# Moving the states' products of a chunked linear attention to another place in the loop, with one PSUM bank shared by sums and outputs

## The chip, the core and the metric

The kernel is one program on one core of a Trainium2 chip. The core has five engines that run side by side: TensorE (PE in the profile; its weight loads are PEld), VectorE (DVE), ScalarE (ACT), GpSimd (POOL) and SyncE (SP), which here issues nearly all DMAs. TensorE writes its results to PSUM, which has eight banks of 512 float32 columns on 128 partitions; DVE and ACT read them from there. The metric is the device time of one execution in microseconds, as the median of several runs.

## The reference

Three stages follow one another. The first is a linear attention with a decay for each token and feature, for 4 batches, 8 heads, 768 tokens and 48 features a head:

```python
for t in range(S):
    state = alpha[:, :, t, :, None] * state + np.einsum('bhd,bhe->bhde', k[:, :, t], v[:, :, t])
    y[:, :, t] = np.einsum('bhd,bhde->bhe', q[:, :, t], state)
```

Its output, as 3072 tokens of 384 features, goes through a soft mixture of 8 experts with 4 slots each (softmax of `x @ phi` over the tokens, `slot_input = d.T @ x`, relu between `w1` and `w2` for each expert, and back to the tokens by a softmax over the slots), and that through a gated MLP with 1536 hidden units (`silu(g) * val @ w_out`). The three MLP matrices arrive as float64 and are made into float32 on the chip, bit by bit.

## The kernel before

**Tiling.** Two heads make a unit, s = 0 on partitions 0 to 63 (48 of them used) and s = 1 on partitions 64 to 111. 4 batches of 4 units give 16 units, each cut into two groups h = 0 and h = 1 of three chunks of 128 tokens. The main loop (`fast`, from L622) runs over these 32 groups g. Within a chunk the attention is a masked product of queries and keys; what came earlier enters through a 48x48 state for each head. A group of h = 0 has no state for its first chunk, so it has 4 products with states, one of h = 1 has 6.

**One round of the loop**, in the order in which PE gets its work (the order is written by hand, the semaphores are set by the framework):

1. `emit_st(g, 1-h)` (L402, L404), a link of the chain of states: the identity times the last state is added on PE to the chunk's sum k'v, and ACT multiplies it with the chunk's total decay into the next state, in SBUF.
2. `emit_s(g+1)` (L353): scores of the next group, into two banks of their own.
3. `emit_st(g, 2-h)`: the second link. Each link needs the state that ACT made from the one before.
4. `emit_kt(g+1)` (L371) transposes the keys, and ACT copies them (L374).
5. `emit_xt(g-1)` (L462) transposes the outputs of the group before; ACT copies them (L466). Then `emit_masks(g+1)`: DVE (L360), ACT (L362) and POOL (L363) mask the scores.
6. `emit_l(g-1)` (L453): logits of the experts' slots from those outputs.
7. `emit_past(g)` (L420): the states times the queries, into the bank `y`, one column range of 128 for each chunk. The two heads lie on diagonal quarters of the array: rows 0 to 63 to columns 0 to 63, rows 64 to 111 to columns 64 to 111.
8. `emit_dh(g+1)` (L390): the chunks' sums k'v of the next group, into one of the three banks `m`. With an odd g, `emit_st(g+1, 0)` follows at once; it is ACT's multiplication alone.
9. `emit_ip(g)` (L432): masked scores times v, added onto the same bank `y`; ACT copies all 384 columns to SBUF as x (L434).

Every float32 product stands as two instructions in the trace, so a row with x12 is six products.

**Beside it** DVE and POOL make the decays three groups ahead (L306 to L325), ACT and DVE turn one piece of the float64 weights into float32 in most rounds (`conv_y`, L249 on ACT; `conv`, L253 to L261 on DVE), and after a batch's last unit the slot steps run (`slot_steps`, from L468): a peak on DVE, exponentials on ACT, two transposes and the slots' input on PE, in the rounds that follow.

**Loads.** SP works off one queue in order. Each round it loads keys, queries, decays and values of later groups; a load of the weights w1, then w2, then wo is issued while a credit lasts (840 columns a round, a tile of w1 or w2 is 1536) and while the allocator `Arena` has room. The arena has a part "near" (31600 columns) and a part "far" (19184). A buffer that is no longer needed at the end of the loop goes back to the arena, and neighbours that are free together hold a weight tile. Behind the loop come the last slot steps, the experts' first layer (L853), which frees the w1 tiles, the second layer (L910), which needs all of w2, and the MLP (L1006 to L1045).

PSUM's eight banks are `m` three times, `s` twice, and `y`, `l` and `r` once.

Of the kernel before, what the change touches and what calls it, by code (L numbers as in the profile page):

```python
# [8 lines left out]
F32 = mybir.dt.float32  # L9
# [9 lines left out]
CH = 128  # L19
# [3 lines left out]
NU = H // 2  # L23
NE, NSL, FE = 8, 32, 1024
# [7 lines left out]
BLK = 1536  # L32
SEL = {0: 2, 1: 3, 3: 4, 4: 5}
LAST = 4
GV0, RATE = 1, 840
TINY = 2.0 ** -55
NEAR, ROUND = 31600, 19184
LA = 3


# [52 lines left out]
def attention_slots_mlp(ctx: ExitStack, tc: tile.TileContext, kq, at, vt, phi, w1, w2, wgv, wo, cst, out):  # L93
    nc = tc.nc
# [9 lines left out]
    mask = cs[:, 128:256]  # L104
    sel = cs[:, 256:288]
    negm = cs[:, 288:289]
    phs = const.tile([112, NU, NSL], F32, name="phs")
    tots = const.tile([112, B * NU, NC], F32, name="tots")
    pall = const.tile([96, 385], F32, name="pall")
    nmx = const.tile([96, 4], F32, name="nmx")  # L110
# [30 lines left out]
    def program(general):  # L141
# [13 lines left out]
        z_g = zone(2, 2 * GP, 0)  # L155
        z_c = [(ar.alloc(GP, 0), GP)]

        zn = {nm: [0] * n for nm, n in (("a", 4), ("p", 5), ("v", 4), ("w", 2), ("x", 2))}
        zsize = {"a": HW, "p": HB, "v": 288, "w": HW, "x": 384}
        for z in "a0 a1 p2 a2 p3 v0 w0 a3 p4 v1 w1 p0 v2 p1 v3 x0 x1".split():  # L160
            zn[z[0]][int(z[1])] = ar.alloc(zsize[z[0]], 1)
        z_a, z_p, z_v, z_w, z_x = (zn[nm] for nm in "apvwx")
        z_y = zone(1, 5 * XK)
# [15 lines left out]
        def psm():  # L179
            return ps_m.tile([128, 512], F32, tag="m", name="m")  # L180
# [196 lines left out]
        def new_g():  # L377
            ng[0] += 1
            return gsts[:, ng[0] % 7, :]

        def emit_dh(g):
            n, h = sgs[g]
            vv[g] = have.pop(("v", g))
            v = view(vv[g]).rearrange("p (c e) -> p c e", e=96)
            t = ktok.pop(g)
            dps[g] = psm()
            for c in range(nk(g)):
                for s in range(2):
                    m = 64 if s == 0 else 48
                    nc.tensor.matmul(dps[g][64 * s:64 * s + m, c * 48:c * 48 + 48], lhsT=t[:, c, 64 * s:64 * s + m], rhs=v[:, c, 48 * s:48 * s + 48], start=(c == 0), stop=True, skip_group_check=True)  # L390

        dps = {}


        def emit_st(g, c):
# [9 lines left out]
            if c == nk(g) - 1:  # L405
                del dps[g]

        yps = {}


        def emit_past(g):
            n, h = sgs[g]
            q = view(qp[g], 112)
            yps[g] = ps_y.tile([128, 512], F32, tag="y", name="y")
            for c in range(3):
                cc = 3 * h + c
                o = slice(c * CH, (c + 1) * CH)
                for s in range(2) if cc else ():
                    p = slice(0, 64) if s == 0 else slice(64, 112)
                    nc.tensor.matmul(yps[g][p, o], lhsT=gst[n, cc][p, 0:p.stop - p.start], rhs=q[p, o], start=(cc == max(1, 3 * h)), stop=False, skip_group_check=True)  # L420
            del qp[g]
            release(pair.pop(g), z_p, g + 5)

        def emit_ip(g):
            n, h = sgs[g]
            v = view(vv[g]).rearrange("p (c e) -> p c e", e=96)
            ps = yps[g]
            for c in range(3):
                o = slice(c * CH, (c + 1) * CH)
                for s in range(2):  # L430
                    p = slice(0, 64) if s == 0 else slice(64, 112)
                    nc.tensor.matmul(ps[p, o], lhsT=v[:, c, 48 * s:48 * s + p.stop - p.start], rhs=smk[g, s][:, c], start=False, stop=True, skip_group_check=True)  # L432
            xt[g] = (z_x.pop(0), 384)
            nc.scalar.copy(view(xt[g], 112), ps[0:112, 0:384])  # L434
            del smk[g, 0], smk[g, 1], yps[g]
            release(vv.pop(g), z_v, g + 4)

        def release(r, z, g):
            if g < NSG:
# [5 lines left out]
        def emit_l(g):  # L445
            n, h = sgs[g]
            b, u = units[n]
            if u == 0 and h == 0:
                lps[b] = ps_l.tile([128, 512], F32, tag="l", name="l")
            x = view(xt[g], 112)  # L450
            for j in range(3):
                t0 = j * CH
                nc.tensor.matmul(lps[b][32 * j:32 * j + 32, CH * h:CH * h + CH], lhsT=phs[:, u, :], rhs=x[:, t0:t0 + CH], start=(u == 0 and h == 0), stop=(u == NU - 1), skip_group_check=True)  # L453

        def emit_xt(g, between=lambda: None):
            n, h = sgs[g]
# [11 lines left out]
        def slot_steps(b):  # L468
# [27 lines left out]
            def e_tok():  # L496
# [3 lines left out]
                st["et"] = st["e2"][:, 0:192].rearrange("p (r e) -> p r e", r=2)  # L500
                nc.vector.tensor_copy(st["et"].rearrange("p r e -> p (r e)"), ps[:, 0:192])

            def part(between=lambda: None):
                ps = psm()
                o = NU * b % 5
                pieces = [(0, o, min(NU, 5 - o))] + [(5 - o, 0, NU - 5 + o)] * (o > 1)
                for r in range(2):
                    if r:
                        between()
                    for u, p, w in pieces:  # L510
                        for j in range(3):
                            nc.tensor.matmul(ps[32 * j:32 * j + 32, 96 * u:96 * u + 96 * w], lhsT=st["et"][:, r, 32 * j:32 * j + 32], rhs=xtok[:, p:p + w, 3 * r + j, :], start=(r == 0 and u == 0), stop=(r == 1), skip_group_check=True)
                if own:
                    for c in (slice(0, 128), slice(128, 384)):
                        nc.scalar.copy(pb[:, c], ps[0:96, c])
                else:
                    nc.vector.scalar_tensor_tensor(out=pall[:, 0:384], in0=pall[:, 0:384], scalar=fac, in1=ps[0:96, 0:384], op0=ALU.mult, op1=ALU.add)
                    nc.vector.scalar_tensor_tensor(out=pall[:, 384:385], in0=pall[:, 384:385], scalar=fac, in1=den, op0=ALU.mult, op1=ALU.add)
                if b == B - 1:
                    drop((z_y[0], 5 * XK))  # L520
# [56 lines left out]
        def fast():  # L577
# [11 lines left out]
            calm, cold[0] = cold[0], view((z_g[0], 256)).bitcast(BF16)  # L589
            nc.gpsimd.memset(cold[0], 0.0)  # L590

            keep_warm(10)
            cold[0] = calm
            nc.vector.memset(rst, 0.0)
            nc.vector.memset(least, TINY)
# [9 lines left out]
            scan_w(1)  # L605
            scale(1, 0, nc.gpsimd)
            scan_p(1)
            keep_warm(4)
            scale(1, 1, nc.vector)
            emit_masks(0)  # L610
            emit_dh(0)
# [4 lines left out]
            scale(2, 0, nc.gpsimd)  # L616
            scale(2, 1, nc.vector)
            pump_units()
            keep_warm(6)
            pend = []  # L620
            credit[0] = 0
            for g in range(NSG):  # L622
                n, h = sgs[g]
                nxt = g + 1 < NSG

                emit_st(g, 1 - h)
                if GV0 < g and (g <= 8 or g % 8 not in (3, 4)):
                    conv_y()
                if g + 3 < NSG:
                    scan_w(g + 3, lambda: conv(0))  # L630
                    scan_p(g + 3)
# [12 lines left out]
                if g:  # L644
                    emit_xt(g - 1)
                if nxt:
                    emit_masks(g + 1)
                    del kp[g + 1]
                    pump_units()
                late = False  # L650
                if g:
                    emit_l(g - 1)
                    release(xt.pop(g - 1), z_x, g + 1)
                    p = sgs[g - 1][0]
                    if sgs[g - 1][1] == 1 and units[p][1] == NU - 1:
                        pend += slot_steps(units[p][0])
                        late = True
                        pend.pop(0)()
                if pend and not late:
                    pend.pop(0)()  # L660
                emit_past(g)
                if nxt:
                    emit_dh(g + 1)
                    if h:
                        emit_st(g + 1, 0)
                conv(2)
                emit_ip(g)
                if late:
                    pend.pop(0)()
                    pend.pop(0)()  # L670
                if gvd[0] == NG and z_c:
                    done_c()

                pump_gv()
                credit[0] = min(credit[0] + RATE, 2 * BLK)
                reserve[0] = 6 - len(gvb)
                while credit[0] > 0:
                    c = credit[0]
                    pump(1)
                    if credit[0] == c:  # L680
                        break
                pump_units()
            for r in z_t:
                drop(r)
            assert few[1] is not None
# [443 lines left out]
def _arrays(q, k, v, alpha, moe_phi, moe_w1, moe_w2, moe2_w_gate, moe2_w_val, moe2_w_out):  # L1129
# [14 lines left out]
        for i in range(NC):  # L1144
            at[:, :, 64 * s:64 * s + 48, 129 * i + 1:129 * i + 129] = a[:, :, s, :, i]
    vt = c(v.reshape(B, NU, 2, NC, CH, D).transpose(0, 1, 4, 3, 2, 5)).reshape(B, NU, CH, NC * 96)
    ph = np.zeros((112, NU, NSL), np.float32)
    pr = moe_phi.reshape(NU, 2, D, NSL)
    for s in range(2):
        ph[64 * s:64 * s + 48] = pr[:, s].transpose(1, 0, 2)  # L1150
# [31 lines left out]
```

## Time and profile before

| | |
|---|---|
| median of 3 runs | 389.02 us (388.72 to 393.24) |
| the profiled execution, its own time | 390.72 us |
| its span in the trace | 389.0 us |
| mean granted clock of TensorE | 0.987 |
| main loop, first to last scores after the start | about 24 to 148 us |
| experts and the last loads of w2 | about 156 to 188 us |
| MLP | about 199 to 382 us |

The span is the time from the first to the last instruction of the program in the trace. Each engine's rows give start and duration; PE's matmuls are pipelined, so that the row of one stage reaches into the next, and the distance from the start of a stage to the start of the next is the time that it costs. A value in square brackets behind a row is the idle time of the engine before it, and what ended it.

### The profile page before, as it was taken

The page shows a single profiled execution, that of the slowest core. Times are in us where ns is not written, and L with a number is a line of the kernel's source. Part 1 is how long each engine was busy: PE and PEld are TensorE (multiplying, and loading weights), DVE is VectorE, ACT ScalarE, POOL GpSimd, SP SyncE. Part 2 cuts the span into 40 slices and gives each one's busy share as a digit, 9 for nine tenths or more (in the row PEclk, how much of TensorE's full clock was granted, in tenths as well). Part 3 has the DMA queues.
Part 4 walks back from the last instruction along what each step waited for, and adds up shares of the span by engine and source line. Part 5 has one row for each costly group of instructions (what it writes and reads, how often), then busy time and mean ns, then how long its engine had stood idle before and what let it go on. Part 6 is the DMA issues. An engine that isn't in the chain of part 4 may idle for free.

```text
span 389.0 us, 8609 instructions
## 1 busy us (share of the span) xinstructions
PE 371.4 (95%) x3308; PEld 278.9 (72%) x3309; DVE 291.2 (75%) x566; ACT 201.2 (52%) x468; POOL 100.8 (26%) x105
## 2 busy tenths in 40 slices
PE   7799999999999999899899999999999999999992
PEld 3577777777777776434368868888888888888881
DVE  6969997999999973215789987677777867877550
ACT  2256665666456565523376755445455545446441
POOL 3347875685588641010300000000000000000000
PEclk9879999999999999999999999999999999999998
DMA  8969999899899959899900004204204114112002
GB/s 273 352 221 329 373 352 356 289 340 345 275 346 363 336 164 354 298 345 412 401 30 0 3 27 125 73 3 150 71 2 153 40 33 152 37 36 82 3 1 90
DMA packets 28627, 74.25 MB, mean 191 GB/s; under 512 B 3216, under 2 KB 11648, under 8 KB 28576
## 3 DMA queue, kind: packets, MB, share of 16 engines
q1 hardware_dynamic: 28256, 73.27, 53.3%
q8 instruction: 28, 0.46, 0.5%
q10 hardware_dynamic: 272, 0.21, 0.2%
q14 instruction: 23, 0.19, 0.2%
q0 software_dynamic: 48, 0.13, 0.1%
HBM read 68.87 MB, written 4.72 MB: 189 GB/s over the span
## 4 chain that ended last, share of the span: by engine, by line
PE 81%; DVE 6%; DMA 3%; ACT 2%; issue 2%; POOL 1%; SPq 0%; DVEq 0%; ACTq 0%; POOLq 0%
PE m L1045 22%; PE acc L1045 11%; PE s L353 6%; PE y L432 6%; PE y L420 6%; PE s L1006 4%; PE m L402 4%; PE s L1007 4%; PE m L390 3%; PE m L371 3%; PE l L453 3%; DMA near<-w 3%; PE s L853 3%; PE m L462 2%; DVE near L1012 1%
## 5 line engine op out<-in xcount | busy, mean ns | idle before, releaser
L1045 PE MATMUL m<-rnd 128*128 128x512 f32 x432 | 129.2, 389 | 0.0
L1045 PEld LDWEIGHTS m<-rnd 128*128 128x128 f32 x432 | 81.1, 188 | 16.8
L1009 ACT ACTIVATE near<-s 128x512 f32<-128x512 f32 x72 | 43.1, 599 | 79.0 <-PE s L1006 77.3
L1045 PE MATMUL acc<-rnd 128*128 128x512 f32 x216 | 81.1, 392 | 0.7 <-DVE rnd L901 0.7
L325 POOL TENSOR_TENSOR far<-far 112x384 f32<-112x384 f32 x61 | 74.5, 1240 | 8.8 <-DVE far L307 4.7
L1012 DVE TENSOR_TENSOR near<-near,s 128x512 f32<-128x512 f32 x72 | 49.3, 685 | 36.1 <-ACT near L1009 35.9
L1020 DVE TENSOR_TENSOR rnd<-near,rnd 128x512 fp32r<-128x512 f32 x72 | 49.4, 686 | 3.2 <-ACT rnd L1018 3.1
L1045 PEld LDWEIGHTS acc<-rnd 128*128 128x128 f32 x216 | 40.5, 188 | 10.3 <-DVE rnd L901 1.6
L1018 ACT CAST rnd<-near 128x512 fp32r<-128x512 f32 x72 | 44.3, 616 | 0.2 <-DVE near L1012 0.2
L404 ACT ACTIVATE far<-m,tots 112x48 f32<-112x48 f32 x80 | 24.3, 304 | 26.7 <-PE m L402 14.6
L307 DVE TENSOR_TENSOR_SCAN far<-far,r 112x388 f32<-112x388 f32 x32 | 30.8, 962 | 5.1 <-DMA far<-at 2.4
L353 PE MATMUL s<-far 64*128 64x128 f32 x384 | 30.8, 293 | 3.5 <-POOL far L325 2.2
L363 POOL TENSOR_SCALAR_AFFINE_SELECT far<-far 128x384 f32<-128x384 f32 x32 | 20.2, 631 | 47.3 <-ACT far L362 47.3
L1116 DVE TENSOR_REDUCE amm<-near 112x1 f32<-112x768 f32 x32 | 30.3, 946 | 2.5 <-DMA near<-at 2.5
L314 DVE TENSOR_TENSOR_SCAN far<-far,r 112x387 f32<-112x387 f32 x32 | 30.7, 959 | 1.1
L257 DVE SCALAR_TENSOR_TENSOR near<-near 128x384 uint32<-128x384 uint32 x36 | 21.6, 599 | 11.3 <-ACT near L249 10.3
L434 ACT COPY far<-y 112x384 f32<-112x384 f32 x32 | 15.3, 480 | 28.3 <-PE y L432 28.3
L353 PEld LDWEIGHTS s<-far 64*128 64x128 f32 x384 | 24.7, 191 | 6.1 <-POOL far L325 4.5
L432 PE MATMUL y<-far 128*48 128x128 f32 (+1 forms) x384 | 28.9, 276 | 0.0
L1006 PE MATMUL s<-rnd 128*128 128x512 f32 x72 | 28.3, 393 | 0.0
L1007 PE MATMUL s<-rnd 128*128 128x512 f32 x72 | 28.1, 391 | 0.0
L420 PE MATMUL y<-far 48*48 48x128 f32 (+1 forms) x320 | 24.9, 283 | 0.0
(163 smaller groups left out, 493.4 us busy)
## 6 DMA issues: line engine op xcount, KB each, us to landing
near<-w SPq DMA_DIRECT2D x18, 768.0 KB, 7.3
far<-kq SPq DMA_DIRECT2D x32, 384.0 KB, 5.1
far<-w SPq DMA_DIRECT2D x14, 768.0 KB, 6.3
near<-wgv SPq DMA_DIRECT2D x24, 384.0 KB, 5.8
far<-at SPq DMA_DIRECT2D x32, 194.0 KB, 5.0
near<-at SPq DMA_DIRECT2D x16, 339.1 KB, 3.3
far<-vt SPq DMA_DIRECT2D x32, 144.0 KB, 4.6
near<-wo SPq DMA_DIRECT2D x12, 384.0 KB, 8.0
```

Source lines behind the costliest of these rows:

```text
L307: nc.vector.tensor_tensor_scan(w[:, ::-1], a[:, ::-1], rst[:, ::-1], 0.0, ALU.mult, ALU.add)
L325: eng.tensor_tensor(out=xv, in0=xv, in1=sv, op=ALU.mult)
L353: nc.tensor.matmul(sps[g][s][:, o:o + CH], lhsT=k[64 * s:64 * s + 64, t0:t0 + CH], rhs=q[64 * s:64 * s + 64, t0:t0 + CH], start=True, stop ...
L420: nc.tensor.matmul(yps[g][p, o], lhsT=gst[n, cc][p, 0:p.stop - p.start], rhs=q[p, o], start=(cc == max(1, 3 * h)), stop=False, skip_group_ ...
L432: nc.tensor.matmul(ps[p, o], lhsT=v[:, c, 48 * s:48 * s + p.stop - p.start], rhs=smk[g, s][:, c], start=False, stop=True, skip_group_check ...
L1006: nc.tensor.matmul(pg, lhsT=swk[n][:, 128 * o:128 * o + 128], rhs=ctT[t % 4], start=True, stop=True)
L1007: nc.tensor.matmul(pv, lhsT=swk[n][:, 256 + 128 * o:256 + 128 * o + 128], rhs=ctT[t % 4], start=True, stop=True)
L1009: nc.scalar.activation(sg, pg, AF.Silu)
L1012: nc.vector.tensor_tensor(out=h_, in0=sg, in1=pv, op=ALU.mult)
L1018: nc.scalar.copy(hi, h_)
L1020: nc.vector.tensor_tensor(out=lo, in0=h_, in1=hi, op=ALU.subtract)
L1045: nc.tensor.matmul(p, lhsT=passes[j][0][:, sl], rhs=passes[j][1], start=(f == 0 and j == 0), stop=(f == NF - 1 and j == 2))
```

## The change

The products with the states move. Instead of standing between the logits and the next group's sums in round g, `emit_past(g)` now stands in round g+1, right behind the first link `emit_st(g+1, ...)`, and ahead of the scores. `emit_ip` now comes first and opens the output, `emit_past` adds to it and ends with the copies to SBUF.

The middle chunk of each group (c = 1) gets its output in a bank `m` of its own, with the two heads swapped: head 0 goes from rows 0 to 63 to columns 64 to 111, head 1 from rows 64 to 111 to columns 0 to 63. Chunks 0 and 2 stay in the bank `y`. ACT copies the output to x with two instructions (128 and 256 columns) instead of one. What reads x undoes the swap: the logits take a second copy of phi with the heads swapped, the slots' input reads the two heads in the other order.

The chunks' sums k'v (`dps`), which had a bank `m`, now lie in columns 256 to 399 of the same bank `y` that takes the outputs of the group before.

Besides: one buffer for x instead of two (the far part is 128 columns smaller, since phi's second copy takes 128 columns elsewhere); the conversion of weights starts in round 1 instead of 2; and once the units' loads are all issued, the credit for weight loads is no longer 840 a round but without limit; the warming matmuls use a bank `m`.

```diff
-GV0, RATE = 1, 840
+RATE = 840
-NEAR, ROUND = 31600, 19184
+NEAR, ROUND = 31600, 19056
...
+        def new_y():
+            ybank[0] = ps_y.tile([128, 512], F32, tag="y", name="y")
+            return ybank[0]
...
-            dps[g] = psm()
+            dps[g] = new_y()[:, 256:400]
...
+        def swap(c):
+            return int(c == 1 and not general)
+        def half(s):
+            return slice(0, 64) if s == 0 else slice(64, 112)
+        def y_out(g, s, c):
+            return yps[g][c == 1][half(s ^ swap(c)), CH * (c // 2):CH * (c // 2) + CH]
+        def emit_ip(g):
+            cleared = g + 1 < NSG
+            yps[g] = ybank[0] if cleared else new_y(), psm()
+            v = view(vv[g])
+            for c in range(3):
+                for s in range(2):
+                    o = y_out(g, s, c)
+                    e = 96 * c + 48 * s
+                    nc.tensor.matmul(o, lhsT=v[:, e:e + o.shape[0]], rhs=smk[g, s][:, c], start=(c == 1 or c == 0 and not cleared), stop=True, skip_group_check=True)
+            del smk[g, 0], smk[g, 1]
+            release(vv.pop(g), z_v, g + 4)
...
         def emit_past(g):
             n, h = sgs[g]
             q = view(qp[g], 112)
-            yps[g] = ps_y.tile([128, 512], F32, tag="y", name="y")
             for c in range(3):
                 cc = 3 * h + c
                 for s in range(2) if cc else ():
+                    o = y_out(g, s, c)
+                    nc.tensor.matmul(o, lhsT=gst[n, cc][half(s), 0:o.shape[0]], rhs=q[half(s), c * CH:(c + 1) * CH], start=False, stop=True, skip_group_check=True)
+            xt[g] = (z_x.pop(0), 384)
+            x = view(xt[g], 112)
+            y, z = yps.pop(g)
+            nc.scalar.copy(x[:, CH:2 * CH], z[0:112, 0:CH])
+            nc.scalar.copy(x.rearrange("p (c t) -> p c t", t=CH)[:, 0::2], y[0:112, 0:2 * CH].rearrange("p (c t) -> p c t", t=CH))
             del qp[g]
             release(pair.pop(g), z_p, g + 5)
...
                 emit_st(g, 1 - h)
-                if GV0 < g and (g <= 8 or g % 8 not in (3, 4)):
-                    conv_y()
+                if g:
+                    emit_past(g - 1)
+                    if g <= 8 or g % 8 not in (3, 4):
+                        conv_y()
...
-                emit_past(g)
                 if nxt:
                     emit_dh(g + 1)
...
-                credit[0] = min(credit[0] + RATE, 2 * BLK)
+                credit[0] = min(credit[0] + RATE, 2 * BLK) if uloads else NEAR
...
+            emit_past(NSG - 1)
```

More of the change, by code (lines that the diff above doesn't have):

```diff
@@ L106, in attention_slots_mlp @@
     negm = cs[:, 288:289]
-    phs = const.tile([112, NU, NSL], F32, name="phs")
+    phs = const.tile([112, 2, NU, NSL], F32, name="phs")
     tots = const.tile([112, B * NU, NC], F32, name="tots")
@@ L156, in program @@
         z_c = [(ar.alloc(GP, 0), GP)]
-        zn = {nm: [0] * n for nm, n in (("a", 4), ("p", 5), ("v", 4), ("w", 2), ("x", 2))}
+        zn = {nm: [0] * n for nm, n in (("a", 4), ("p", 5), ("v", 4), ("w", 2), ("x", 1))}
         zsize = {"a": HW, "p": HB, "v": 288, "w": HW, "x": 384}
-        for z in "a0 a1 p2 a2 p3 v0 w0 a3 p4 v1 w1 p0 v2 p1 v3 x0 x1".split():
+        for z in "a0 a1 p2 a2 p3 v0 w0 a3 p4 v1 w1 p0 v2 p1 v3 x0".split():
             zn[z[0]][int(z[1])] = ar.alloc(zsize[z[0]], 1)
@@ L379, in new_g @@
             return gsts[:, ng[0] % 7, :]
+        dps, yps, ybank = {}, {}, [None]
+        def new_y():
+            ybank[0] = ps_y.tile([128, 512], F32, tag="y", name="y")
+            return ybank[0]
         def emit_dh(g):
@@ L390, in emit_dh @@
                     nc.tensor.matmul(dps[g][64 * s:64 * s + m, c * 48:c * 48 + 48], lhsT=t[:, c, 64 * s:64 * s + m], rhs=v[:, c, 48 * s:48 * s + 48], start=(c == 0), stop=True, skip_group_check=True)
-        dps = {}
         def emit_st(g, c):
@@ L406, in emit_st @@
                 del dps[g]
-        yps = {}
+        def swap(c):
[15 more added lines that the diff above has]
+            release(vv.pop(g), z_v, g + 4)
         def emit_past(g):
@@ L413, in emit_past @@
             q = view(qp[g], 112)
-            yps[g] = ps_y.tile([128, 512], F32, tag="y", name="y")
             for c in range(3):
                 cc = 3 * h + c
-                o = slice(c * CH, (c + 1) * CH)
                 for s in range(2) if cc else ():
-                    p = slice(0, 64) if s == 0 else slice(64, 112)
-                    nc.tensor.matmul(yps[g][p, o], lhsT=gst[n, cc][p, 0:p.stop - p.start], rhs=q[p, o], start=(cc == max(1, 3 * h)), stop=False, skip_group_check=True)
+                    o = y_out(g, s, c)
[5 more added lines that the diff above has]
+            nc.scalar.copy(x.rearrange("p (c t) -> p c t", t=CH)[:, 0::2], y[0:112, 0:2 * CH].rearrange("p (c t) -> p c t", t=CH))
             del qp[g]
             release(pair.pop(g), z_p, g + 5)
[L424 to L436, printed above, removed]
         def release(r, z, g):
@@ L452, in emit_l @@
                 t0 = j * CH
-                nc.tensor.matmul(lps[b][32 * j:32 * j + 32, CH * h:CH * h + CH], lhsT=phs[:, u, :], rhs=x[:, t0:t0 + CH], start=(u == 0 and h == 0), stop=(u == NU - 1), skip_group_check=True)
+                nc.tensor.matmul(lps[b][32 * j:32 * j + 32, CH * h:CH * h + CH], lhsT=phs[:, swap(j), u, :], rhs=x[:, t0:t0 + CH], start=(u == 0 and h == 0), stop=(u == NU - 1), skip_group_check=True)
         def emit_xt(g, between=lambda: None):
@@ L501, in e_tok, with x_rows @@
                 nc.vector.tensor_copy(st["et"].rearrange("p r e -> p (r e)"), ps[:, 0:192])
+            def x_rows(p, w, r, j):
+                x = xtok[:, p:p + w, 3 * r + j, :]
+                if swap(j):
+                    x = bass.AP(x.tensor, x.offset + 48, [list(x.ap[0]), list(x.ap[1]), [-48, 2], [1, 48]])
+                return x
             def part(between=lambda: None):
@@ L511, in part @@
                         for j in range(3):
-                            nc.tensor.matmul(ps[32 * j:32 * j + 32, 96 * u:96 * u + 96 * w], lhsT=st["et"][:, r, 32 * j:32 * j + 32], rhs=xtok[:, p:p + w, 3 * r + j, :], start=(r == 0 and u == 0), stop=(r == 1), skip_group_check=True)
+                            nc.tensor.matmul(ps[32 * j:32 * j + 32, 96 * u:96 * u + 96 * w], lhsT=st["et"][:, r, 32 * j:32 * j + 32], rhs=x_rows(p, w, r, j), start=(r == 0 and u == 0), stop=(r == 1), skip_group_check=True)
                 if own:
@@ L590, in fast @@
             nc.gpsimd.memset(cold[0], 0.0)
-            keep_warm(10)
+            keep_warm(10, psm())
             cold[0] = calm
@@ L607, in fast @@
             scan_p(1)
-            keep_warm(4)
+            keep_warm(4, psm())
             scale(1, 1, nc.vector)
@@ L618, in fast @@
             pump_units()
-            keep_warm(6)
+            keep_warm(6, psm())
             pend = []
@@ L652, in fast @@
                     emit_l(g - 1)
-                    release(xt.pop(g - 1), z_x, g + 1)
+                    release(xt.pop(g - 1), z_x, g)
                     p = sgs[g - 1][0]
@@ L1146, in _arrays @@
     vt = c(v.reshape(B, NU, 2, NC, CH, D).transpose(0, 1, 4, 3, 2, 5)).reshape(B, NU, CH, NC * 96)
-    ph = np.zeros((112, NU, NSL), np.float32)
+    ph = np.zeros((112, 2, NU, NSL), np.float32)
     pr = moe_phi.reshape(NU, 2, D, NSL)
     for s in range(2):
-        ph[64 * s:64 * s + 48] = pr[:, s].transpose(1, 0, 2)
+        for x in range(2):
+            ph[64 * s:64 * s + 48, x] = pr[:, s ^ x].transpose(1, 0, 2)
     w1 = c(moe_w1.reshape(NE, 3, 128, 2, 512).transpose(0, 3, 2, 1, 4)).reshape(NE, 2, 128, BLK)
```

## The prediction

> **What bounds the kernel now.** I read the page's busy times, then the stretches, then the timeline of PE and ACT over two rounds, and the chain of waits where the loop ends.
>
> ```profile
> core 0: us, PE busy (x) PEld busy (x) DVE busy (x) ACT busy (x) POOL busy (x), PEclk, DMA share, GB/s
> 10.00:20.00 10.00, 7.77 (x81) 5.87 (x80) 9.29 (x21) 2.60 (x9) 3.34 (x4) 0.84 0.99 345
> 20.00:30.00 10.00, 10.00 (x130) 7.64 (x128) 6.93 (x15) 5.39 (x16) 5.17 (x6) 0.82 0.64 214
> 180.00:190.00 10.00, 8.34 (x97) 3.20 (x89) 8.72 (x16) 3.54 (x8) 3.55 (x3) 1.00 1.02 408
> 24.30:148.23 123.93, 122.36 (x1855) 94.28 (x1851) 113.05 (x254) 75.78 (x221) 85.02 (x82) 1.00 0.91 317
> ```
>
> In the main loop PE is busy for 122.36 of 123.93 us, DVE for 113.05, ACT for 75.78. So whatever lengthens PE's order lengthens the loop, and what shortens it meets DVE some 9% further down. The loop's rounds can be counted on the chain, whose first and last scores of this stretch are these:
>
> ```profile
> 24.37 0.87 PE s L353 x12
> ...
> 148.30 0.87 PE s L353 x12
> ```
>
> They are the scores of groups 3 and 31: 28 rounds, 14 pairs of an even and an odd one. PE's stages over one pair:
>
> ```profile
> 103.83 0.31 PE L402 MATMUL m<-far,cs 64*64 64x48 f32 x4
> 104.08 0.94 PE L353 MATMUL s<-far 64*128 64x128 f32 x12
> ...
> 106.17 0.65 PE L420 MATMUL y<-far 64*64 64x128 f32 x8
> 106.74 0.43 PE L390 MATMUL m<-far 128*64 128x48 f32 x8
> 106.96 0.88 PE L432 MATMUL y<-far 128*48 128x128 f32 x12
> 107.78 0.31 PE L402 MATMUL m<-far,cs 64*64 64x48 f32 x4
> ```
> ```profile
> 108.02 0.94 PE L353 MATMUL s<-far 64*128 64x128 f32 x12
> 108.89 0.31 PE L402 MATMUL m<-far,cs 64*64 64x48 f32 x4
> ...
> 109.85 0.42 PE L453 MATMUL l<-far,phs 112*32 112x128 f32 x6
> 110.20 0.87 PE L420 MATMUL y<-far 64*64 64x128 f32 x12
> 111.00 0.49 PE L390 MATMUL m<-far 128*64 128x48 f32 x11
> 111.31 0.28 PE L432 MATMUL y<-far 128*48 128x128 f32 x1
> ...
> 112.14 0.31 PE L402 MATMUL m<-far,cs 64*64 64x48 f32 x4
> 112.39 0.38 PE L353 MATMUL s<-far 64*128 64x128 f32 x2
> ```
>
> No row has an idle time before it. From scores to scores it is 3.94 us with four products of states (L420 x8) and 4.37 with six (x12), 8.31 a pair. The states' products cost 106.74 − 106.17 = 0.57 and 111.00 − 110.20 = 0.80: two more pairs of instructions cost 0.23, so 0.11 for each pair that runs at once, and 0.14 for entering and leaving the stage.
>
> **The change, part by part.**
>
> *Products leave their old place.* Logits to sums is then the 0.35 that logits to products take now (109.85 to 110.20): −0.57 −0.80 = −1.37 a pair.
>
> *Products behind the first link.* The framework that sets the semaphores keeps order between engines by the whole PSUM tile, which is a bank. The link's sum, which ACT has to read, and the outputs of chunks 0 and 2, which PE has to write, now lie in one tile. So I take it that PE's products wait until ACT's multiplication is through. Before has no two engines at work on different columns of one tile, so its trace doesn't show this wait; it shows what such a turn costs:
>
> ```profile
> 109.25 0.30 ACT L404 ACTIVATE far<-m,tots 112x48 f32<-112x48 f32 x1 [0.23 <-PE m L402]
> ...
> 110.35 0.50 ACT L362 COPY far<-s 128x384 f32<-128x384 f32 x1
> 111.60 0.30 ACT L404 ACTIVATE far<-m,tots 112x48 f32<-112x48 f32 x1 [0.75 <-PE m L390]
> ```
> ```profile
> 151.92 0.31 PE L402 MATMUL m<-far,cs 64*64 64x48 f32 x4
> 152.78 0.31 PE L402 MATMUL m<-far,cs 64*64 64x48 f32 x4 [0.55 <-ACT far L404]
> ```
> ```profile
> 152.42 0.32 ACT far L404
> ```
>
> A link that starts at 108.89 has its multiplication start 0.36 later; that takes 0.30; and in the last round (the second and third fence, PE's timeline and the chain), where no scores lie between, PE goes on at 152.78, 0.04 to 0.05 after ACT's end. So PE may write 0.36 + 0.30 + 0.05 = 0.71 after the link's start. The scores, which hid this turn before (they follow the link after 0.24), now stand behind the products.
>
> The bounds are no wait at all and this 0.71; I take the 0.71, since the tile is one and the nearest row pays the turn in full. [...]
>
> What runs after the wait: with six products, chunks 0 and 1 are on four different quarters. If four go at once, three chunks take 4 steps of 0.11 plus 0.14 = 0.58, and scores begin 0.71 + 0.58 = 1.29 after the link instead of 0.25 (112.39 − 112.14): +1.04. If only pairs go at once it is 0.80, +1.26. With four products the middle chunk comes first in the order; its bank is free of ACT, so it runs inside the wait, and the last chunk takes 2 steps: 0.71 + 0.36 = 1.07 instead of 0.24: +0.83. I take the four: the rows above already show two row halves at once (L353, 64 rows each, 12 instructions in 0.87), two column halves (L390) and the diagonal (L420). [...]
>
> *Sums in the outputs' bank.* With an odd g the sums of g+1 are followed by ACT's multiplication of the first state, and then by `emit_ip(g)`, whose first product goes to the same bank. Before, L432 starts 0.31 after L390. Now it waits: ACT starts 111.60 − 111.00 = 0.60 after the sums' start, plus 0.30 and 0.05: 0.95, so +0.64 a pair. Behind it on PE stands all of `emit_ip`; nothing else is there to run. Bounds: 0 and 0.64; I take 0.64 for the same reason.
>
> Sum for a pair: −1.37 + 1.04 + 0.83 + 0.64 = +1.14; for 14 pairs +16.0.
>
> *ACT's copies.* One copy of 384 columns (0.48) becomes two; between rows of 0.30 for 48 columns and 0.48 for 384, 128 and 256 columns are some 0.34 and 0.41: +0.27 a round, on an engine with 75.78 of 123.93 us busy. They lie behind the scores' 0.87, end before the second link needs the bank, and cost nothing. Without that cover it would be 0.27 x 28 = 7.6. The swapped reads of x and phi's second copy are the same instructions on the same number of columns: 0.
>
> *Slot rounds.* After three batches the exponentials stand ahead of the link's multiplication on ACT:
>
> ```profile
> 88.56 0.31 PE L402 MATMUL m<-far,cs 64*64 64x48 f32 x4
> ...
> 90.33 0.31 PE L402 MATMUL m<-far,cs 64*64 64x48 f32 x4 [0.58 <-ACT far L404]
> ```
>
> PE then goes on 1.77 after the link. Before, the scores covered all but 0.58 of it. Now the products wait for it, 1.77 − 0.71 = 1.06 longer than in my pair, and the 0.58 goes: +0.48, three times, +1.4.
>
> *Start and end.* Up to 24 us the loop waits for DVE and POOL, and the clock is 0.84 and 0.82 in the two stretches: between 0 and 2, I take +0.5. The last round has no scores: it gains the removed stage and loses the wait, 0.
>
> *Loads.* Freeing one x buffer puts a fourth w1 tile into the far part, so one tile more fits everywhere; the conversion that starts a round earlier takes its last piece out of SP's way. In the allocator's order of frees, the tile of w2 that is now issued at 171.84 comes with the three before it. Behind the loop the DMAs bound the end of the experts:
>
> ```profile
> 171.84 0.33 SPq L236 DMA_DIRECT2D near<-w  x1
> 172.22 1.46 SPq L238 DMA_DIRECT2D near<-wo  x3
> 175.12 1.95 SPq L236 DMA_DIRECT2D near<-w  x4
> ```
> ```profile
> 176.68 11.37 DMA near<-w
> ```
>
> What is issued from 171.84 on lands until 188.05. A tile less there is 0.79 MB at 408 GB/s, 1.9 us: bounds −4 (two tiles) and 0, I take −1.9. The issue itself hangs on L853, so on the end of the loop; it doesn't absorb the delay.
>
> Sum: 16.0 + 1.4 + 0.5 − 1.9 = +16.0. Against the profiled span of 389.0 this gives 405.0; that execution's own time was 390.72, 1.7 over the median of 389.02, which itself is the span's number, so I predict a median of 405.0.
>
> **The rivals.**
>
> *Pairs only.* The swapped quarters don't run beside the diagonal ones: +0.22 in each of 14 odd groups, 408. For it: no row with four. Against: both kinds of halves at once in the rows.
>
> *ACT becomes late.* L374, the copy of the transposed keys, is what the sums need; with the products gone from ahead of them only the logits cover it:
>
> ```profile
> 109.72 0.44 ACT L374 COPY far<-m 128x336 f32<-128x336 f32 x1 [0.17 <-PE m L371]
> ```
>
> It ends at 110.16, the sums could start at 110.20. If the two copies and the conversion push it back by 0.2 in every round, 28 x 0.2 = 5.6 more, 411. Against: ACT waits 0.17 before it today.
>
> *No waits (the other side).* Accesses to other columns of the bank are let through. Then the products follow the link in the same kind of tiles, 0.44 and 0.22 for 4 and 2 steps, and a pair changes by −1.37 + 0.66 = −0.71. PE comes to 122.36 − 9.9 = 112.4, just under DVE's 113.05, so the loop loses about 9; with −1.9 behind it, 378. It decides at waits of under 0.71 a pair; my waits are the difference of the two sums, 1.14 + 0.71 = 1.85. Against: it would need two engines at one bank.
>
> *Waits half of mine*, for instance because only one of the two turns is ordered: −0.71 + 0.93 = +0.22 a pair, 3 us over the loop, which with the start's 0.5, the slot rounds at half (0.7) and the loads' −1.9 gives 391, within 2%.
>
> **How the numbers follow.** Forecast 0.66, pairs only 0.15, ACT late 0.08, no waits 0.06, short waits 0.05. 2% of 389 is 7.8 us, about what a measurement of this kernel can tell from no change. Faster by more is the no-wait case, 0.06; within is the short-wait case, 0.05; slower is the rest, 0.89. The range takes the bounds of the tail (−4 to 0), the start (0 to 2), half of a wait in the odd rounds (−4), and reaches over pairs only: 399 to 410.
>
> **What would show it.** Right: L420 has an idle time of some 0.3 to 0.5 us before it, ended by ACT L404 or its successor; the first link to the scores is about 1.3 and 1.1 us; the products of `emit_ip` in odd rounds wait some 0.6 for ACT; pairs of rounds take about 9.45 instead of 8.31; DVE's busy share falls; the last w2 lands earlier counted from the end of the loop. Wrong: products that start right behind the link without idle time; six products that take 0.8; an idle time before the sums ended by the copy of the keys; a clock below 1.00 in the loop, which the stretch from 180 to 190 (8.34 of 10 us busy, 1.00) speaks against.

## Result, and the profile after

| | before | after |
|---|---|---|
| median | 388.87 us of 4 runs (388.2 to 393.24) | 415.45 us of 4 runs (410.01 to 421.84) |
| ratio | 1 | 1.0526 (95%: 1.0442 to 1.061) |
| profiled execution: own time, span | 390.72, 389.0 | 411.45, 409.7 |
| scores of group 3 to scores of group 31 | 123.93 | 145.98 |
| from there to the end | 240.8 | 240.1 |

The changed kernel is slower by some 5%. Two of its four executions ran at a lower mean granted clock (0.955 and 0.946 instead of 0.987 and 0.982); here and below a ratio is to the kernel before, run beside it, without the executions that lie more than 1.5% above the fastest of their kernel, while a median is that of all.

The lines of the code have moved a little: the scores are still L353 and the copy of the keys L374, the sums are now L396, the link is L406 with ACT's multiplication L408, `emit_ip` is L433, `emit_past` L444, the logits L468. The conversion on ACT is still L249.

The loop as one stretch (the view by stretches, with the columns of the prediction's first fence):

```profile
core 0: us, PE busy (x) PEld busy (x) DVE busy (x) ACT busy (x) POOL busy (x), PEclk, DMA share, GB/s
23.62:169.60 145.98, 126.02 (x1852) 91.64 (x1850) 113.94 (x258) 79.53 (x249) 79.17 (x82) 0.98 0.85 289
```

PE is busy for about as long as before, 126.02 us against 122.36, but the stretch is 22.05 us longer: PE now stands still for 20 us of it, where it had stood for 1.6. One pair of rounds in PE's timeline shows where (start, duration, and in brackets the idle time before the row and what ended it):

```profile
116.63 0.94 PE L353 MATMUL s<-far 64*128 64x128 f32 x12
...
119.75 0.25 PE L406 MATMUL y<-far,cs 64*64 64x48 f32 x2
119.76 0.33 PE L444 MATMUL m<-far 64*48 64x128 f32 x2
...
120.47 0.43 PE L444 MATMUL y<-far 64*64 64x128 f32 x4 [0.27 <-ACT far L408]
120.83 0.94 PE L353 MATMUL s<-far 64*128 64x128 f32 x12
...
123.03 0.55 PE L396 MATMUL y<-far 128*64 128x48 f32 x12
123.98 0.43 PE L433 MATMUL y<-far 128*64 128x128 f32 x4 [0.41 <-ACT far L408]
...
124.78 0.31 PE L406 MATMUL y<-far,cs 64*64 64x48 f32 x4
125.50 0.32 PE L444 MATMUL y<-far 64*64 64x128 f32 x2 [0.41 <-ACT far L408]
125.52 0.33 PE L444 MATMUL m<-far 64*48 64x128 f32 x2
125.66 0.28 PE L444 MATMUL y<-far 48*48 48x128 f32 x2
125.66 0.29 PE L444 MATMUL m<-far 64*48 64x128 f32 x2
...
126.08 0.49 PE L353 MATMUL s<-far 64*128 64x128 f32 x3
```

Three things show here. Scores to scores it is 120.83 − 116.63 = 4.20 and 126.08 − 120.83 = 5.25, so 9.45 for a pair instead of 8.31. All three idle times end with ACT's L408, and what stands behind each is a product that writes the bank `y`; the middle chunk's products, in `m`, start at 119.76 with no idle time, straight behind the link of 119.75. And with six products, those in `y` and those in `m` start together (125.50 and 125.52, then twice 125.66), so four quarters are at work; the stage takes 126.08 − 125.50 = 0.58.

Not all of the 22 us is in these pairs. The first rounds hold another wait, here in the timelines of ACT and PE about the round that starts at 27.82:

```profile
29.83 0.55 ACT L249 ACTIVATE near<-near 128x384 f32<-128x384 f32 x1 [1.46 <-DMA near<-wgv]
30.28 0.29 ACT L408 ACTIVATE far<-y,tots 112x48 f32<-112x48 f32 x1
30.46 0.43 ACT L374 COPY far<-m 128x336 f32<-128x336 f32 x1
```
```profile
29.66 0.42 PE L468 MATMUL l<-far,phs 112*32 112x128 f32 x6
30.95 0.55 PE L396 MATMUL y<-far 128*64 128x48 f32 x12 [0.88 <-ACT far L374]
```

ACT has stood for 1.46 us in a conversion whose piece of weights had not landed. Behind it in ACT's order are the link and the copy of the keys, and PE waits 0.88 us for that copy before the sums. The view of one line's instructions gives what ACT waited for ahead of the conversion (us, times), first after, then before:

```profile
  DMA near<-wgv: 6.2, 7
```
```profile
  DVE near L261: 0.8, 1
```

Seven waits of together 6.2 us for the loads of wgv, where before has none. The third loss is late in the loop, in the view by stretches:

```profile
154.00:158.00 4.00, 2.65 (x38) 1.90 (x35) 2.77 (x7) 1.36 (x5) 2.30 (x3) 0.85 0.64 219
158.00:160.00 2.00, 2.00 (x19) 1.69 (x18) 0.74 (x2) 0.43 (x2) 0.00 (x0) 0.50 0.80 292
160.00:162.00 2.00, 2.00 (x22) 1.34 (x23) 1.06 (x5) 1.12 (x3) 0.39 (x1) 0.50 1.00 406
162.00:164.00 2.00, 1.80 (x22) 1.12 (x18) 0.00 (x0) 0.36 (x2) 1.91 (x3) 0.60 0.19 77
```

For almost 7 us the granted clock is 0.50 (the last section works this out). PE is busy nearly all the time there, but the round of four products takes 6.77 us instead of 4.20.

### The profile page after: what moved, and what is told of

Read it like the earlier page. It is cut to its first block, busy times and chain, and to the rows that moved or that the text cites. A ratio compares the mean times of both kernels' runs of the same rounds, so it can differ in the third digit from the quotient of the medians.

```text
span 409.7 us, 8731 instructions
## 1 busy us (share of the span) xinstructions
PE 374.8 (91%) x3308; PEld 274.6 (67%) x3309; DVE 290.3 (71%) x566; ACT 205.2 (50%) x500; POOL 95.7 (23%) x105
## 4 chain that ended last, share of the span: by engine, by line
PE 71%; DMA 9%; ACT 8%; DVE 7%; issue 3%; SPq 0%; ACTq 0%; DVEq 0%
PE m L1069 21%; PE acc L1069 10%; DMA near<-wgv 6%; PE s L353 5%; PE y L433 4%; PE s L1030 4%; PE s L1031 3%; PE y L444 3%; ACT far L408 3%; PE y L406 3%; DMA near<-w 3%; PE s L877 3%; PE m L371 2%; PE l L468 2%; PE y L396 1%
## 5 line engine op out<-in xcount | busy, mean ns | idle before, releaser
L325 POOL TENSOR_TENSOR far<-far 112x384 f32<-112x384 f32 x61 | 69.2, 1152 | 6.1 <-DMA far<-kq 3.8
L408 ACT ACTIVATE far<-y,tots 112x48 f32<-112x48 f32 x80 | 23.9, 298 | 47.6 <-PE y L406 45.3
L433 PE MATMUL y<-far 128*48 128x128 f32 (+1 forms) x256 | 27.9, 284 | 7.7 <-ACT far L408 7.7
L353 PE MATMUL s<-far 64*128 64x128 f32 x384 | 31.5, 299 | 1.2 <-DVE r L306 1.2
L353 PEld LDWEIGHTS s<-far 64*128 64x128 f32 x384 | 25.2, 195 | 7.4 <-issue 4.4
L444 PE MATMUL y<-far 64*64 64x128 f32 (+1 forms) x192 | 17.6, 289 | 11.5 <-ACT far L408 11.5
L253 DVE TENSOR_SCALAR near<-near 128x384 uint32<-128x384 uint32 x36 | 13.6, 377 | 17.9 <-DMA near<-wo 9.7
## 6 DMA issues: line engine op xcount, KB each, us to landing
far<-kq SPq DMA_DIRECT2D x32, 384.0 KB, 4.3
near<-wgv SPq DMA_DIRECT2D x24, 384.0 KB, 5.1
near<-wo SPq DMA_DIRECT2D x12, 384.0 KB, 9.2
```

Source lines behind the costliest of these rows:

```text
L325: eng.tensor_tensor(out=xv, in0=xv, in1=sv, op=ALU.mult)
L353: nc.tensor.matmul(sps[g][s][:, o:o + CH], lhsT=k[64 * s:64 * s + 64, t0:t0 + CH], rhs=q[64 * s:64 * s + 64, t0:t0 + CH], start=True, stop ...
L408: nc.scalar.mul(gst[n, cc][:, 0:48], ps, tots[:, n, cc:cc + 1])
L433: nc.tensor.matmul(o, lhsT=v[:, e:e + o.shape[0]], rhs=smk[g, s][:, c], start=(c == 1 or c == 0 and not cleared), stop=True, skip_group_ch ...
```

## The experiments

The first theory is the prediction's: the two turns of PE, ACT and PE through the bank `y` make the loop longer. Against it stood, once the traces were there, that the late keys (ACT held up by loads) or the clock carry a large part. The edits are against the changed kernel.

**Sums in a bank of their own (own).** Neither turn is left; the rest of the change stays.

```diff
-            dps[g] = new_y()[:, 256:400]
+            dps[g] = psm()
...
-            cleared = g + 1 < NSG
+            cleared = False
```

> The changed kernel, but the chunks' sums have a bank m of their own again; products stay behind the first link, middle chunk on the swapped quarters. Theory (two waits on ACT by the shared bank): both waits go, a pair of rounds falls from 9.45 to 7.6 on PE, with DVE (113 us of work in 28 rounds, 8.07 a pair) as the next bound, so the stretch from the scores of group 3 to those of group 31 takes 113 to 118 us instead of 146, the span is 376 to 383, and the clock stays at 1.00 in the loop. Rival (the moved place itself or the swapped quarters cost it): pairs stay near 9.4, span 405 to 411.

Measured: median 394.37 (389.53 to 398.17, 10 runs), ratio 1.0068 (1.0014 to 1.0123), profiled span 388.4. PE's timeline:

```profile
105.14 0.94 PE L353 MATMUL s<-far 64*128 64x128 f32 x12
...
108.26 0.25 PE L406 MATMUL m<-far,cs 64*64 64x48 f32 x2
108.27 0.33 PE L444 MATMUL m<-far 64*48 64x128 f32 x2
108.39 0.30 PE L444 MATMUL y<-far 48*48 48x128 f32 x2
108.74 0.94 PE L353 MATMUL s<-far 64*128 64x128 f32 x12
...
110.94 0.49 PE L396 MATMUL m<-far 128*64 128x48 f32 x11
111.25 0.28 PE L433 MATMUL y<-far 128*48 128x128 f32 x1
...
112.78 0.48 PE L353 MATMUL s<-far 64*128 64x128 f32 x3
```

All idle times before L433 and L444 are gone, and a pair takes 7.65 (here 108.74 − 105.14 = 3.60 and 112.78 − 108.74 = 4.04; 4.05 in most rounds): 1.80 less than after and 0.66 less than before. So the waits come from the shared bank, and the moved products alone are a gain for PE. Whether the chip itself needs the turns isn't shown: the framework orders the engines by the tile, and no run lets both at one bank at once. But the span lies above the 376 to 383 that stood in the expectation. The loop still takes 128.25 us. Some 6 us of it are waits before the sums, because the waits for the loads are larger here than in the changed kernel (nine of together 11.4 us); more goes behind the slot steps, where PE stands up to 1.16 us for ACT:

```profile
27.95 0.56 ACT L249 ACTIVATE near<-near 128x384 f32<-128x384 f32 x1 [2.41 <-DMA near<-wgv]
```
```profile
29.08 0.49 PE L396 MATMUL m<-far 128*64 128x48 f32 x11 [1.89 <-ACT far L374]
```

PE gets to these sums at 27.2 us instead of 30.1 and waits 1.89 us there instead of 0.88, for keys whose copy stands behind a load.

**One turn at a time (own_even, own_odd).** Only the sums of the even groups, or only those of the odd ones, get their own bank.

```diff
-            dps[g] = new_y()[:, 256:400]
+            dps[g] = psm() if sgs[g][1] == 0 else new_y()[:, 256:400]
...
-            cleared = g + 1 < NSG
+            cleared = g + 1 < NSG and sgs[g + 1][1] == 1
```

For own_odd the 0 and the 1 change places.

> As the changed kernel, but the sums of even groups have a bank of their own; those of odd groups stay in the outputs' bank. Theory: the wait of emit_ip behind the sums goes (0.64 a pair), and the wait before six products (0.60); the wait before four products stays. Pair of rounds 8.2, span 390 to 394. If only one of the two waits were real, the pair stays at 8.8 or more.

> As the changed kernel, but the sums of odd groups have a bank of their own; those of even groups stay in the outputs' bank. Theory: only the wait before four products goes (0.61 of 0.83 a pair), the other two stay. Pair of rounds 8.8, span 399 to 404.

Measured: own_even 4.20 + 4.05 = 8.25 a pair, own_odd 3.60 + 5.25 = 8.85. One pair of own_even in PE's timeline:

```profile
121.14 0.94 PE L353 MATMUL s<-far 64*128 64x128 f32 x12
...
125.18 0.94 PE L353 MATMUL s<-far 64*128 64x128 f32 x12
...
129.02 0.43 PE L444 MATMUL y<-far 64*64 64x128 f32 x4 [0.27 <-ACT far L408]
129.38 0.94 PE L353 MATMUL s<-far 64*128 64x128 f32 x12
```

So the odd round pays 1.20 for the shared bank (the turn before `emit_ip` and the one before six products), the even round 0.60 (the turn before four products), and the two parts, 1.80, add up to what own took away. The times bear less: own_even took 405.85 and 393.23 us at mean clocks of 0.960 and 0.995, own_odd 408.69 and 410.83 (ratio 1.0514, 1.042 to 1.0608) at 0.956 and 0.952. For both the profiled span (404.1 and 409.0) lies above the 390 to 394 and 399 to 404 that followed from the pairs; the clock in the loop is 0.90 in both.

**The conversion a round later (conv2).** It starts in round 2, as it did before; both turns stay. Now two pieces are loaded ahead of the first conversion instead of one.

```diff
-                    if g <= 8 or g % 8 not in (3, 4):
+                    if g > 1 and (g <= 8 or g % 8 not in (3, 4)):
```

> The changed kernel with one edit: the weights' conversion starts in round 2 again instead of 1. Theory: rounds 4 and 8 lose the waits of 0.88 and 1.14 us before the sums (ACT stands in the conversion until its piece of wgv has landed, and the copy of the keys stands behind it), L249 no longer waits for the DMA near<-wgv, pairs stay at 9.45: span 2 to 4 us shorter, 405 to 408. Rival (the copies of x make ACT late by themselves): the waits before the sums stay, span as before this edit.

Measured: median 405.02 (404.66 and 405.38), ratio 1.0392 (1.0306 to 1.0479), span 402.9. The same place as in the fences about 27.82 above, and then the loop, in PE's timeline and by stretches:

```profile
28.28 0.42 PE L468 MATMUL l<-far,phs 112*32 112x128 f32 x6
28.64 0.55 PE L396 MATMUL y<-far 128*64 128x48 f32 x12
```
```profile
22.24:162.57 140.33, 122.83 (x1852) 89.50 (x1850) 111.55 (x254) 80.19 (x249) 80.86 (x83) 1.00 0.88 300
```

The wait before the sums is gone in all 28 rounds of the loop, a pair is still 9.45, and the clock is 1.00 through the loop. It is 5.65 us shorter than that of the changed kernel. Round by round those 5.65 are 0.93 and 1.20 in the two rounds with a wait before the sums, 0.60 in the two after the second one, and 2.93 in the two rounds at half clock. So the early start of the conversion costs about 2.7 directly. For the clock, the two kernels were run once more in one go.

**The same two again (after_again, conv2_again).** No edit.

> The changed kernel itself, more executions beside the next one on one chip. Theory (its conversion, a round too early, makes ACT wait for pieces of wgv, and these longer idle times of PE let the clock fall in some executions): executions from 408 to 422, mean clock from 0.945 to 0.99.

> The changed kernel with the conversion from round 2, more executions. Theory: 404 to 407 in every execution, mean clock 0.985 or more. Rival (the waits by the shared bank, which are all still there, let the clock fall by themselves): as far apart as the changed kernel.

Measured: 407.31, 414.14, 414.72 and 429.73 us for the changed kernel, at mean clocks of 0.989, 0.973, 0.979 and 0.928; with the later conversion 404.43 to 409.01 (4 runs, ratio 1.0453, 1.039 to 1.0516), at 0.980 to 0.993. Both are spread wider than expected. Over both occasions eight executions of the one reach from 407.31 to 429.73, six of the other from 404.43 to 409.01. The half clock falls on other rounds each time; in this profile of the changed kernel (span 412.4) its longest spell is here:

```profile
52.00:56.00 4.00, 3.49 (x32) 2.67 (x34) 3.83 (x9) 0.96 (x5) 2.65 (x3) 0.50 0.82 302
56.00:60.00 4.00, 4.00 (x40) 3.02 (x38) 2.01 (x5) 2.19 (x7) 0.48 (x1) 0.50 0.78 259
60.00:64.00 4.00, 3.85 (x44) 2.72 (x41) 3.34 (x9) 2.23 (x8) 2.43 (x3) 0.72 0.27 55
```

In these executions the early start goes together with a lower and less steady clock, though the least disturbed ones of the changed kernel (407.31, 410.01 and 411.45) come close to the others. That the waits for the loads set off the drops isn't shown: the drop near 157 us in the first profile lies far behind the last such wait, at 65.70, and own_conv2 below has drops without any.

**Useless products in the waits (conv2_warm).** On top of conv2, one bf16 product of 128 by 512 that nobody reads is put into each of the two turns.

```diff
+                    keep_warm(1, psm())
                     emit_past(g - 1)
...
+                if h:
+                    keep_warm(1, psm())
                 emit_ip(g)
```

> The changed kernel with the conversion from round 2, and one bf16 matmul of 128x512 without use (0.22 to 0.38 us) in each of the waits: behind the link, and ahead of emit_ip in odd rounds. Theory (PE's idle time in the waits lets the clock fall to half in some executions): the waits are filled, pairs grow by 0 to 0.2, and no stretch of the loop has a clock below 1.00 in any run; the runs lie within 1% of one another. Rival (the clock falls for another reason): runs as far apart as those of the changed kernel, with clocks down to 0.95.

Measured: median 405.76 (405.36 to 406.16, 4 runs), ratio 1.0405 (1.0364 to 1.0446), pairs of 9.45, mean clocks of 0.991 to 0.994. The time is that of conv2 (405.02). It costs nothing to fill the turns, so they are waiting time and no work of PE; for the clock it tells nothing, as conv2 was already steady.

**Without the swap (noswap).** The middle chunk keeps its own bank but its products stay on the diagonal quarters.

```diff
-            return int(c == 1 and not general)
+            return 0
```

> The changed kernel, but the middle chunk's heads are not swapped, so that all products lie on the diagonal quarters, the middle chunk still in its own bank. Theory (four quarters at once are worth a pair of steps, 0.22, for six products; for four products the middle chunk runs inside the wait anyway): from scores to scores 5.25 becomes 5.47 and 4.20 stays; span 2 to 4 us longer, apart from the clock. Rival (the quarters don't run beside one another): 5.25 stays.

Measured: median 419.69 (418.94 and 420.44), ratio 1.0762 (1.0704 to 1.082), span 418.7. PE's timeline over one odd round:

```profile
131.73 0.94 PE L353 MATMUL s<-far 64*128 64x128 f32 x12
...
136.40 0.43 PE L444 MATMUL y<-far 64*64 64x128 f32 x4 [0.41 <-ACT far L408]
136.67 0.39 PE L444 MATMUL m<-far 48*48 48x128 f32 x4
136.88 0.39 PE L444 MATMUL y<-far 48*48 48x128 f32 x4
137.20 0.49 PE L353 MATMUL s<-far 64*128 64x128 f32 x4
```

The bank `m` now comes between the two of `y` instead of beside them. The round takes 137.20 − 131.73 = 5.47 instead of 5.25, the even one is still 4.20. So the swap is worth the 0.22 that the prediction had given to two steps. The rest of this kernel's time is again waits before the sums (up to 1.92 us) and the clock of 0.968.

**Both cures (own_conv2), and the same without the swap (own_conv2_noswap).** The edits of own and conv2 together; then that of noswap as well.

> Both edits at once: sums in a bank of their own and the conversion from round 2. Theory (waits by the shared bank, and waits of ACT for pieces of wgv that land too late): pairs of 7.65 as with the own bank, and no wait before the sums, which summed to 5 to 6 us there: span 381 to 385, 1 to 2% below the kernel before; PE idles too little in the loop for the clock to fall, so the runs lie close together. Rival (DVE, 8.07 us of work a pair, is the bound by now): the waits go elsewhere and the span stays at 387 to 389.

> Sums in a bank of their own, conversion from round 2, heads not swapped. Without waits the swap should be worth 0.22 in both kinds of rounds: 3.60 becomes 3.82 and 4.05 becomes 4.27, 6 us over 28 rounds; less of it in the span, 2 to 4 us over the kernel with the swap, if DVE bounds part of the loop.

Measured: own_conv2 385.51 (384.66 to 387.22, 4 runs), ratio 0.9878 (0.9838 to 0.9919); without the swap 387.25 (386.06 to 389.32, 7 runs), ratio 0.9926 (0.9889 to 0.9963), with rounds of 3.81 and 4.26. So with these two parts taken back, the products in their new place do make the kernel faster, by 1.2%: little, but the interval doesn't reach 1. The intervals of the two kernels overlap, so that on time the swap isn't told apart: 1.7 us between the medians, where 2 to 4 were expected. A pair of 7.65 in own_conv2 should have shortened the loop by 14 x 0.66 = 9.2 us; it went from 123.93 to 122.81. By stretches:

```profile
84.00:88.00 4.00, 2.84 (x34) 1.86 (x33) 3.83 (x10) 3.27 (x12) 1.79 (x3) 0.86 0.99 364
88.00:92.00 4.00, 4.00 (x57) 3.32 (x58) 3.83 (x10) 1.61 (x5) 2.56 (x3) 0.71 0.76 272
...
22.39:145.20 122.81, 116.92 (x1852) 88.80 (x1851) 111.72 (x255) 78.17 (x249) 92.70 (x83) 0.97 0.95 333
```

DVE is busy for 111.72 of the 122.81 us, and for 3.83 of 4.00 about the slot rounds. PE has gaps there, and soon after the one of 1.16 us in the first of these stretches the clock falls (0.86 and 0.71 in the means of the two). Two rounds behind slot steps take 7.07 and 7.60 us; without the swap, where the clock was 1.00 through the loop of the profile, they take 5.54 and 5.55. One wait before the sums is left against the expectation, 0.82 us in another round; there ACT stands 1.41 us in its conversion, and what it waits for is DVE.

**Useless products in those rounds (own_conv2_warm).** Two to four of them ahead of the second link of three rounds.

```diff
+                if g in (9, 17, 25):
+                    keep_warm(2 if g == 9 else 4, psm())
                 emit_st(g, 2 - h)
```

> Sums in a bank of their own and the conversion from round 2, plus 2, 4 and 4 bf16 matmuls of 128x512 without use behind the scores of rounds 9, 17 and 25, where PE idles up to 1.2 us for the exponentials and the clock then falls to 0.86, 0.71 and 0.57 in stretches of 4 us. Theory (idle of about a microsecond is what lets the clock fall): the clock stays at 1.00 there, the rounds that took 7.06 and 7.60 take 4.8 to 5.3, span 380 to 383. Rival (the clock falls anyway, or DVE bounds these rounds): 385 and more.

Measured: median 384.52 (383.37 to 386.21, 4 runs), ratio 0.9868 (0.9832 to 0.9904). The 380 to 383 of the expectation is a span: the profiled execution lies above it with 384.5, the other three within it with 381.6 to 383.0. In own_conv2 the profiled span was 385.5, the others 382.9 to 384.0.

```profile
84.00:88.00 4.00, 3.39 (x51) 2.22 (x49) 3.87 (x9) 1.90 (x9) 4.00 (x5) 1.00 1.04 349
88.00:92.00 4.00, 4.00 (x70) 3.18 (x66) 3.83 (x10) 3.10 (x11) 3.16 (x4) 1.00 1.01 387
```

The clock is 1.00 where it had been 0.86 and 0.71, and the two long rounds come to 5.31 each, some 4 us less together. Yet the loop as a whole is only 2.45 us shorter (120.36 instead of 122.81): other rounds take 1.6 us more. The profiled span fell by 1.0 alone, since this loop happened to begin 1.5 us later, ahead of any edited round. The 1.6 that other rounds lose fit DVE as the bound (3.87 and 3.83 of 4.00 here); it isn't shown, since no run made DVE's work lighter. With a clock of 1.00 on both sides, the loop with the swap (120.36) is 2.8 us shorter than the one without it (123.15).

**The old credit (own_conv2_cred).** On top of own_conv2, to see whether the loads without limit earn anything.

```diff
-                credit[0] = min(credit[0] + RATE, 2 * BLK) if uloads else NEAR
+                credit[0] = min(credit[0] + RATE, 2 * BLK)
```

> Sums in a bank of their own and the conversion from round 2, with the old credit of 840 columns a round also behind the last unit's load. If the credit without limit is worth something, it shows behind the loop: the tile of w2 that now starts early comes later, and the stretch from the scores of group 31 to the end grows by 0 to 2 us. I expect under 1, since the second layer of the experts waits for the last four tiles, whose loads hang on the first layer.

Measured: median 384.63 (383.54 to 387.23, 5 runs), ratio 0.9878 (0.9838 to 0.9918). From the last scores to the end it is 239.6 us with the old credit and 240.3 with the new one. The new credit earns nothing.

## Why the prediction was right, and where it was not

*The pair.* Forecast +1.14, measured 9.45 − 8.31 = +1.14, and each term as it was put: link to scores 1.30 (forecast 1.29) and 1.08 (1.07), sums to `emit_ip` 0.95 (0.95). The turn of 0.71 that was read off the last round of the trace before, where no scores lay between link and link, was the right price (125.50 − 124.78 = 0.72 after). That it is the shared bank which makes it is shown by own, own_even and own_odd.

*Four quarters at once.* Right by the rows at 125.50 to 125.66, whose stage takes the 0.58 that was forecast, and by noswap, where it takes 137.20 − 136.40 = 0.80. The rival with pairs only falls.

*No waits, half of them.* Both fall: all three places wait. The rival without waits had its mechanism in own_conv2, whose pairs changed by −0.66 where it had −0.71. But its time of 378 was too low by 7.5, since it let the loop sink to DVE's busy time; the loop stopped at 122.81, with DVE busy for 91% of it.

*Slot rounds.* Forecast +1.4. In conv2, where nothing else disturbs, the loop grew by 140.33 − 123.93 = 16.4, and 16.0 of it are the pairs: +0.4. In two rounds of conv2 that carry slot steps the products wait 0.61 for ACT instead of 0.27, so 0.34 more where 1.06 was forecast three times; a loss that had no term is the wait before `emit_ip`, which three times is 0.95 instead of 0.41, because exponentials of the slot steps (L552) stand ahead of L408 on ACT.

*ACT's copies.* They take 0.26 and 0.37 where 0.34 and 0.41 were put, and no product of the 28 rounds waits for them, as forecast.

*Start.* Forecast +0.5 within 0 to 2; the first of the counted scores came 0.7 earlier in the changed kernel and 2.1 earlier in conv2. Outside of the bounds, on the fast side.

*Loads.* Forecast −1.9 behind the loop; measured −0.7 (240.8 to 240.1), −0.4 in conv2. The loads of w2 that wait for the end of the first layer take nearly as long as before, where it was 11.37; the chain of waits after:

```profile
197.86 11.05 DMA near<-w
```

*What was missed.* The forecast was +16.0, and the profiled span grew by 20.7. Start (−1.2 against the forecast) and loads (+1.2) cancel; the loop was forecast at 16.0 + 1.4 = 17.4 longer and came to 22.05. Without its two disturbances it would have been 16.4, as in conv2; the other 5.65 had no term.

The first of the two is the step on the earlier conversion, which was counted as a help ("takes its last piece out of SP's way"). The conversion now runs one piece behind its load instead of two, and a piece takes 5.1 us from issue to landing (the median), about a round. In ACT's rows that wait stands ahead of the link and of the keys. The rival in which ACT becomes late through L374 had named the place, but put it down to ACT's own work and to every round; it was a load, and only in the early rounds, up to the first ones that convert nothing.

The second is the clock. The prediction held that a PE busy for 8.34 of 10 us keeps its clock, and named a clock below 1.00 in the loop as a sign against itself. That sign came: it fell to 0.50 in a stretch of 4 us with PE busy for 2.65. What set it off stays open.

By the ratio, 1.0526 x 389 = 409.5, the time is at the upper edge of the range of 399 to 410; the median of all four runs, 415.45, lies above it. That the ratio still falls inside is in part luck: the 5.65 had no term, and the room for it was left for the rival with pairs only, which fell. In conv2, which has the predicted mechanism without the early conversion, the median is 405.02 (407.0 in the second four runs), where 405.0 was forecast. So close a fit is luck too: against the forecast its loop is 1.0 shorter, its start 2.6 earlier and its end 1.5 longer, which makes a span of 402.9, and the forecast had taken a span for a time.

## What to carry to other kernels

Here two engines that worked on different columns of one PSUM bank took turns. Price each such turn from a place in the trace where nothing covers it (here 0.71 us from PE through ACT and back), and look what work is queued behind the waiting product. Ask of a conversion in the order of a busy engine how far ahead its load is issued: here, one piece ahead instead of two, it held up the work behind it for some 2.7 us in all. And when a resource is shared to save space, try the move without the sharing: here the move without it is worth 1.2% (own_conv2) and the sharing costs 5% (conv2 against own_conv2).

## What the runs showed of the hardware

The granted clock fell to 0.50 for some microseconds and came back to 1.00. In the first profile of the changed kernel the clock lost between 154 and 164 us is (0.15 x 4 + 0.50 x 2 + 0.50 x 2 + 0.40 x 2) / 0.50 = 6.8 us at half clock; in slices of 0.4 us it is 0.50 from 157.0 to 163.4, and 0.72 and 0.74 in the slices on either side. In own_conv2, between 84 and 92 us, it is (0.14 x 4 + 0.29 x 4) / 0.50 = 3.4; in the second profile of the changed kernel, between 52 and 64 us, (0.50 x 4 + 0.50 x 4 + 0.28 x 4) / 0.50 = 10.2. The 3.4 and the last part of the 10.2 are estimates from the means of stretches of 4 us. The 6.8 and the 3.4 came with stretches of 4 us in which PE was busy for 2.65 and 2.84 us, its longest single idle times there being 0.95 and 1.16 us. Short gaps close together don't always come with a fall: conv2 has the same gaps of 0.27 to 0.95 us and kept 1.00 through the loop of its profile (22.24 to 162.57), and the first profile of the changed kernel kept it where PE was busy for less and had an idle time of 1.14 us:

```profile
49.50:53.50 4.00, 2.07 (x35) 1.38 (x34) 3.48 (x9) 2.32 (x7) 1.75 (x2) 1.00 0.92 320
```

What decides between the two stays open.
